# An attention, SwiGLU and bilinear kernel: front for the first batch alone, pack and unpack both one batch ahead

## The chip, the cores and the metric

The kernel runs on one core of one Trainium2 chip. TensorE (PE in the rows, PEld for its weight loads) multiplies, VectorE (DVE), ScalarE (ACT) and GpSimd (POOL) do the element-wise work, SyncE (SP) issues the DMAs. Each engine works through its own list of instructions in the written order and waits on semaphores for the others. The metric is the device time of one execution in microseconds (us), the median of several runs; less is better. A profiled execution gives the trace of every instruction.

## The reference

Three layers, one after the other, all outputs in fp32:

```python
def sm_attn(qq, kk, vv):
    s = scale * np.matmul(qq, kk.transpose(0, 1, 3, 2))
    a = np.exp(s - np.max(s, axis=-1, keepdims=True))
    return np.matmul(a / (np.sum(a, axis=-1, keepdims=True) + 1e-09), vv)
p_packed = sm_attn(p, k, v)              # 8 batches, 8 heads, 32 packed rows, 576 tokens, 64 wide
x = sm_attn(q, p_packed, p_packed)       # back to 576 tokens; then x as (4608, 512)
xn = x / np.sqrt(np.mean(x * x, axis=-1, keepdims=True) + 1e-06) * rms_g
g, val = xn @ w_gate, xn @ w_val         # 512 -> 1536
x = (g / (1 + np.exp(-g)) * val) @ w_out # 1536 -> 512
out = ((x @ w1) * (x @ w2)) @ w3 @ w_out2
```

## The kernel before

**Stages.** The first third of the span does attention and the gate and value products, batch by batch, and writes their silu product `hT_d` to memory. The rest (from line 480 on: `w_out`, then the bilinear layer) reads it back; the diff does not touch it.

**What a batch needs.** `pack(b)` (line 170) is the first attention: scores (L181), maximum, Exp (L188), transposes of the weights (L197), the product with `v` (L208), a transpose of it (L220) and two small block-diagonal tiles, `bdP1T` (L224) and `bdG` (L239, made from L234). It has 7 steps; a step ends at each `yield`. `unpack(b)` (line 246) is the second attention: scores against the packed rows (L262), a block transpose on VectorE (L266), maximum (L272), subtraction (L274), Exp on ScalarE (L275), sum (L278), a multiply by the reciprocal on GpSimd (L281), a transpose back (L285), then the sum of squares for the norm (L292, L295, L298, L304) and its reciprocal root (L310, L315, L318), and at last the split of the normed rows into two halves of fp32r precision, `ah` and `al` (the helper of L55 and L56). It has 18 steps. `unpack(b)` needs all of `pack(b)`.

**The dense part.** `dense_units(b)` (line 356) has 48 units. A unit is six matmuls of 128x288 (L376) into one of four PSUM banks `gv`. Units go in pairs: the even one is the gate, whose bank ScalarE reads with Tanh (L382) and VectorE multiplies by one plus that (L383); the odd one is the value, which ScalarE copies (L387) and GpSimd multiplies in (L388). After units 3, 11, 19, 27, 35 and 43 comes `wb_unit` (L337): 8 matmuls that fold the packed rows into the next 256 columns of the weights, and their split into `wbh` (ScalarE) and `wbl` (VectorE), two of each, in turns.

**What sets the order.** It is written out by hand. `planned` runs `dense_units(b)` and after the unit with number n takes one step of `unpack` or `pack` for each n in the tables `UNPACK` and `PACK`. In the loop before, `unpack(b + 1)` and `pack(b + 2)` run beside `dense_units(b)`: packing is two batches ahead, so beside the last loop of this kind, b = 6, there is no packing left. The front, ahead of the first dense loop, takes the steps of `pack(0)`, `pack(1)`, `unpack(0)`, the first `wb_unit` and conversions in the order of a string of letters.

**Conversions.** The weights arrive as 64-bit floats. `convert` makes fp32 of a 128x512 piece: ScalarE takes the high words (L108) and the low words (L109), VectorE shifts (L111) and merges (L112), GpSimd adds (L114). The gate and value weights `w_gv` are 24 such pieces, 512 KB each as loaded; `wb_unit(b, g)` of the first batch needs the first 4(g + 1) of them. Pieces of `w_out` are converted later, two in each loop from b = 1 on. `c_h` and `c_y` have two buffers each. Loads go through SP's queue in the written order; `k` and `q` have two buffers, `v` one, the 64-bit pieces four.

## Time and profile before

| | us |
|---|---|
| median of 3 runs | 1455.12 (1455.07 to 1457.11) |
| the profiled execution, its own time | 1451.91 |
| span of the profiled execution, first to last instruction | 1450.1 |
| TensorE busy in it | 1360.0 (94%) |
| VectorE, ScalarE, GpSimd busy | 795.9, 546.7, 489.9 |
| chain that ended last: TensorE's share of the span | 75% |

Over the whole span TensorE is the engine to look at. The 40 slices of the page, 36 us each, show where it is not busy: in the first two (4 and 5 tenths, then 7), and in a slice at about 480 us (7 tenths). A matmul counts as busy from its start to a modelled end, so idle time of TensorE is read from gaps between matmuls and from windows, not from the busy share alone. Times within the trace are counted from the start of the span.

### The profile page before, as it was taken

What the parts mean: (1) busy time and instruction counts of PE and PEld (TensorE: products, weight loads), DVE (VectorE), ACT (ScalarE), POOL (GpSimd) and SP (SyncE); (2) the same over time, 40 slices, a digit from 0 to 9 for tenths busy, and PEclk for the clock granted to TensorE, in tenths of its full rate; (3) what the DMA queues carried; (4) which work ended last, traced back from release to release, by engine and by line L of the source; (5) the groups of instructions that cost most, each with busy time, mean ns of one, the idle gap of its engine ahead of it and who ended that gap; (6) DMA issues with size and microseconds to landing.
All of it is one profiled execution on the core that took longest, in us unless ns stands there. A gap on an engine that the chain in (4) does not pass through costs nothing.

```text
span 1450.1 us, 22603 instructions
## 1 busy us (share of the span) xinstructions
PE 1360.0 (94%) x8824; PEld 1121.8 (77%) x8824; DVE 795.9 (55%) x1267; ACT 546.7 (38%) x1080; POOL 489.9 (34%) x438
## 2 busy tenths in 40 slices
PE   4579999999999899999999978999999999999988
PEld 2368878778788788888887756888788788788877
DVE  4787576666766557736358844335334433533343
ACT  3455455555555555624245532113112211311211
POOL 2456445445456542201034503322221222222111
PEclk9689999999999999999999999999999999999999
DMA  9854453444222466726349885442642633444263
GB/s 308 296 186 119 160 186 120 154 153 141 75 96 81 153 211 236 229 98 201 121 161 364 313 307 225 167 149 84 238 146 88 237 141 115 179 142 145 92 254 125
DMA packets 65562, 253.65 MB, mean 175 GB/s; under 512 B 7344, under 2 KB 7344, under 8 KB 55344
## 3 DMA queue, kind: packets, MB, share of 16 engines
q1 hardware_dynamic: 65456, 252.21, 49.5%
q8 instruction: 69, 1.13, 0.3%
q14 instruction: 37, 0.30, 0.1%
HBM read 185.08 MB, written 67.11 MB: 174 GB/s over the span
## 4 chain that ended last, share of the span: by engine, by line
PE 75%; DVE 8%; DMA 5%; ACT 3%; issue 3%; POOL 1%; SPq 1%; ACTq 0%; DVEq 0%; POOLq 0%
PE gv L799 22%; PE gv L376 17%; PE at L566 8%; PE gv L772 7%; PE at L772 7%; PE gv L566 6%; PE at L337 2%; DMA hr<-w_d 2%; DMA w<-ws_d 2%; PE at L657 2%; PE gv L657 2%; DVE stage L56 1%; PE at L292 1%; DVE c_t L111 1%; DVE th L383 1%
## 5 line engine op out<-in xcount | busy, mean ns | idle before, releaser
L799 PE MATMUL gv<-xh,w 128*128 128x512 f32 (+1 forms) x1120 | 288.7, 373 | 13.5 <-DMA w<-ws_d 6.1
L55 ACT ACTIVATE hh<-hr 128x512 fp32r<-128x512 f32 (+1 forms) x148 | 91.2, 618 | 421.1 <-DVE hr L767 332.9
L799 PEld LDWEIGHTS gv<-xh,w 128*128 128x128 f32 x1120 | 201.9, 190 | 53.3 <-DMA w<-ws_d 7.4
L388 POOL TENSOR_TENSOR ht<-th,vl 128x288 f32<-128x288 f32 x192 | 163.8, 861 | 178.6 <-ACT vl L387 97.6
L376 PE MATMUL gv<-ah,wbh 128*128 128x288 f32 x768 | 178.6, 314 | 15.9 <-ACT vl L387 12.4
L56 DVE TENSOR_TENSOR hl<-hr,hh 128x512 fp32r<-128x512 f32 (+1 forms) x148 | 140.4, 951 | 63.2 <-ACT hh L55 60.2
L376 PEld LDWEIGHTS gv<-ah,wbh 128*128 128x128 f32 x768 | 122.7, 191 | 67.6 <-issue 27.8
L826 POOL TENSOR_TENSOR u<-u,c 128x512 f32<-128x512 f32 (+1 forms) x40 | 63.5, 1587 | 323.5 <-DVE u L767 323.5
L376 PE MATMUL gv<-al,wbh 128*128 128x288 f32 x768 | 167.2, 299 | 0.0
L767 DVE TENSOR_TENSOR hr<-gv,hr 128x512 f32<-128x512 f32 (+1 forms) x80 | 51.1, 639 | 209.4 <-PE gv L799 209.4
L376 PE MATMUL gv<-ah,wbl 128*128 128x288 f32 x768 | 165.5, 297 | 0.0
L799 PE MATMUL gv<-xl,w 128*128 128x512 f32 (+1 forms) x560 | 162.3, 372 | 0.0
L114 POOL TENSOR_TENSOR c_o<-c_o,c_y 128x512 int32<-128x512 int32 x52 | 72.9, 1402 | 223.1 <-DVE c_o L112 200.6
L376 PEld LDWEIGHTS gv<-al,wbh 128*128 128x128 f32 x768 | 125.1, 190 | 1.1 <-DVE al L56 0.9
L376 PEld LDWEIGHTS gv<-ah,wbl 128*128 128x128 f32 x768 | 124.8, 190 | 0.0
L383 DVE SCALAR_TENSOR_TENSOR th<-th,gv 128x288 f32<-128x288 f32 x192 | 84.3, 445 | 63.1 <-ACT th L382 62.1
L799 PEld LDWEIGHTS gv<-xl,w 128*128 128x128 f32 x560 | 102.6, 191 | 18.4
L566 PE MATMUL at<-hh,wo_h 128*128 128x512 f32 x240 | 94.7, 394 | 7.3 <-ACT hh L55 7.3
L387 ACT ACTIVATE vl<-gv 128x288 f32<-128x288 f32 x192 | 79.3, 413 | 58.5 <-PE gv L376 57.2
L56 DVE TENSOR_TENSOR wbl<-at,wbh 128x512 fp32r<-128x512 f32 x96 | 65.9, 687 | 60.3 <-ACT wbh L55 59.6
L566 PE MATMUL at<-hl,wo_h 128*128 128x512 f32 x240 | 94.8, 395 | 2.3 <-DVE hl L56 2.1
L382 ACT ACTIVATE th<-gv 128x288 f32<-128x288 f32 x192 | 79.4, 413 | 42.9 <-PE gv L376 42.9
(131 smaller groups left out, 2416.2 us busy)
## 6 DMA issues: line engine op xcount, KB each, us to landing
w<-ws_d SPq DMA_DIRECT2D x40, 1792.0 KB, 7.4
hT_d<-ht SPq DMA_DIRECT2D x96, 288.0 KB, 2.5
hr<-hT_d SPq DMA_DIRECT2D x108, 256.0 KB, 4.4
ws_d<-stage SPq DMA_DIRECT2D x16, 896.0 KB, 8.3
w<-in_w_gv_dram SPq DMA_DIRECT2D x24, 512.0 KB, 7.0
w<-in_w_out_dram SPq DMA_DIRECT2D x20, 512.0 KB, 4.5
v<-in_v_dram SPq DMA_DIRECT2D x8, 1152.0 KB, 7.6
q<-in_qT_dram SPq DMA_DIRECT2D x8, 1152.0 KB, 7.0
```

What stands on the lines that cost most here:

```text
L55: nc.scalar.activation(out=hi, in_=src, func=AF.Copy)
L56: eng_lo.tensor_tensor(out=lo, in0=src, in1=hi.bitcast(F32), op=ALU.subtract)
L114: nc.gpsimd.tensor_tensor(out=d, in0=d, in1=shape(y), op=ALU.add)
L376: nc.tensor.matmul(t[:, :HALF], lhsT=w[:, e, 256 * i + 128 * f:256 * i + 128 * f + 128], rhs=x[:, e, HALF * hf:HALF * hf + HALF], start=(n ...
L382: nc.scalar.activation(out=th, in_=t[:, :HALF], func=AF.Tanh, scale=0.5)
L383: nc.vector.scalar_tensor_tensor(out=th, in0=th, scalar=1.0, in1=t[:, :HALF], op0=ALU.add, op1=ALU.mult)
L387: nc.scalar.activation(out=vl, in_=t[:, :HALF], func=AF.Copy, scale=0.5)
L388: nc.gpsimd.tensor_tensor(out=ht[:, hf], in0=th, in1=vl, op=ALU.mult)
L566: nc.tensor.matmul(acc[m], lhsT=w[:, kk, 128 * m:128 * m + 128], rhs=x, start=(kk == 0 and a == 0), stop=(kk == NF - 1 and a == 2))
L772: nc.tensor.matmul(acc[m], lhsT=x[:, 128 * m:128 * m + 128], rhs=w[i], start=(i == 0 and n == 0), stop=(i == 7 and n == 2))
L799: nc.tensor.matmul(t, lhsT=wi[:, r, j, a], rhs=x[b][:, j, r, :w], start=(start and n == 0), stop=(n == 5), skip_group_check=True)
L826: nc.gpsimd.tensor_tensor(out=u2, in0=u2, in1=c22, op=ALU.mult)
```

## The change

Five things change, all in the attention and dense stage. Line numbers below are of the kernel before; in the one after, everything from `convert` on stands 4 to 24 lines later.

1. A conversion is two steps: `widened` (the two ScalarE instructions) and `joined` (the two of VectorE and the one of GpSimd). For `w_gv` they are called apart, by `gv_widen` and `gv_join`; a widened piece waits in `c_h` and `c_y`. `wb_unit` no longer converts what is missing, it takes it as converted.
2. The front has only `pack(0)`, `unpack(0)` and the first `wb_unit`, with 9 pieces widened and 8 joined; the letters a and b stand for these two.
3. `pack(b + 1)` runs beside `dense_units(b)`, ahead of `unpack(b + 1)` in the same loop, with new tables; the loop b = 6 has a `pack` now. The 16 joins left run at even distances in the first dense loop. The two conversions of `w_out` in each later loop move from units 21 and 35 to 26 and 38.
4. Loads: two pieces of `w_gv` instead of three ahead of `v`, `k(b + 2)` in every `pack`, `q(b + 1)` right behind `v(b + 1)` in `pack(b)`.
5. An Exp on a 128x2 tile at the start, so that ScalarE's table is loaded there.

```diff
-    def convert(dst, w, shape):
+    def widened(w):
...
         nc.scalar.activation(out=h, in_=w[:, :, 1].bitcast(F32), func=AF.Copy, scale=float(2.0 ** -112))
         nc.scalar.activation(out=y, in_=w[:, :, 0].bitcast(U32), func=AF.Copy, scale=float(2.0 ** -29))
+        return h, y
+
+    def joined(dst, hy, shape):
+        h, y = hy
...
+    def gv_widen():
+        i = len(gvhy)
+        if i < len(GV):
+            gvhy.append(widened(gv64[i]))
+            gv_load(1)
...
-        if b:
-            load_k(b + 2)
+        load_k(b + 2)
...
         load_v(b + 1)
+        load_q(b + 1)
...
-        while not all((g, c) in converted for c in range(NC)):
-            next(gvw)
+        assert all((g, c) in converted for c in range(NC))
...
-    next(gvw)
+    gv_load(2)
     load_v(0)
     load_q(0)
+    gv_load(2)
     load_k(1)
+    warm = att.tile([128, 2], F32, name="warm")
+    nc.scalar.activation(out=warm, in_=ones, func=AF.Exp)
...
-    front = dict(p=chained(pack(0), pack(1)), u=unpack(0), c=gvw, w=wb_first(), l=later())
-    for x in "pp c c p c pp c pp u c u u p u p u c w u u u c u uu p u c uu l pp c uu c uu pp c l c c":
...
+    front = dict(p=pack(0), u=unpack(0))
+    for x in "a pp b a p b pp pp u uu uu aa uu b u b u uu a u w b a u u b a uu uu b a b a":
...
-    PACK = [8, 8, 16, 31, 32, 40, 43]
-    UNPACK = [0, 1, 3, 4, 6, 11, 13, 15, 17, 24, 24, 25, 31, 32, 40, 41, 42, 44]
+    PACK = [0, 0, 8, 10, 10, 12, 16]
+    UNPACK = [17, 18, 18, 19, 20, 21, 22, 23, 24, 32, 33, 33, 37, 37, 41, 42, 43, 44]
...
-        others = [(UNPACK, unpack(b + 1))]
-        if b + 2 < B:
-            others.insert(0, (PACK, pack(b + 2)))
+        others = [(PACK, pack(b + 1)), (UNPACK, unpack(b + 1))]
```

**Where instructions move.** Three places. First VectorE in the front, from the product with `v` to the first transposes of `unpack(0)`; `c_t` and `wgv` are a conversion's two VectorE instructions, `p` is the packed product, `bdP1T`, `gP1T` and `bdG` the small tiles of `pack(0)`, `a` the scores of `unpack(0)`. Before:

```order
L216 TENSOR_SCALAR p_243<-at,rs 128x64 x2
L111 TENSOR_SCALAR c_t<-c_h 128x512
L112 SCALAR_TENSOR_TENSOR wgv<-c_h,c_t 128x2x256
L224 COPY bdP1T<-at 64x4x32 x2
L226 TENSOR_TENSOR gP1T<-at,gT 128x128
L239 COPY bdG<-at 32x2x32 x4
L266 STREAM_TRANSPOSE a_275<-at 128x2x288 x2
```

The same place after:

```order
L241 TENSOR_SCALAR p_241<-at,rs 128x64 x2
L249 COPY bdP1T<-at 64x4x32 x2
L251 TENSOR_TENSOR gP1T<-at,gT 128x128
L264 COPY bdG<-at 32x2x32 x4
L291 STREAM_TRANSPOSE a_263<-at 128x2x288 x2
```

The conversion between `p` and `bdP1T` is gone from the chain.

Second VectorE in a later dense loop, b = 2 before and b = 1 after, where the scores of `unpack` are worked on: `a` the scores, `mx` their maximum, `rs` their sum, `th` the gate of a unit, `wbl` the split of a `wb_unit`. Before:

```order
L266 STREAM_TRANSPOSE a_2307<-at 128x2x288 x2
L272 TENSOR_REDUCE mx_2308<-a_2307 128x18
L383 SCALAR_TENSOR_TENSOR th<-th,gv 128x288
L274 TENSOR_TENSOR a_2307<-a_2307,mx_2308 128x576
L56 TENSOR_TENSOR wbl<-at,wbh 128x512 x2
L383 SCALAR_TENSOR_TENSOR th<-th,gv 128x288
L272 TENSOR_REDUCE mx_2308<-a_2307 128x18
L383 SCALAR_TENSOR_TENSOR th<-th,gv 128x288
L274 TENSOR_TENSOR a_2307<-a_2307,mx_2308 128x576
```

After:

```order
L291 STREAM_TRANSPOSE a_1703<-at 128x2x288 x2
L405 SCALAR_TENSOR_TENSOR th<-th,gv 128x288
L295 TENSOR_REDUCE mx_1704<-a_1703 128x18
L297 TENSOR_TENSOR a_1703<-a_1703,mx_1704 128x576
L295 TENSOR_REDUCE mx_1704<-a_1703 128x18
L56 TENSOR_TENSOR wbl<-at,wbh 128x512 x2
L405 SCALAR_TENSOR_TENSOR th<-th,gv 128x288
L297 TENSOR_TENSOR a_1703<-a_1703,mx_1704 128x576
L301 TENSOR_REDUCE rs_1705<-a_1703 128x18
```

There are two gates of units between the first maximum and the second subtraction's end where three stood, and three passes over the scores stand in a row ahead of the `wbl` of a `wb_unit`.

Third ScalarE at the same two places; `a` is the Exp of half of the scores, `vl` the value of a unit, `wbh` the split of a `wb_unit`. Before:

```order
L382 ACTIVATE th<-gv 128x288
L387 ACTIVATE vl<-gv 128x288
L275 ACTIVATE a_2307<-a_2307 128x576
L55 ACTIVATE wbh<-at 128x512 x2
L382 ACTIVATE th<-gv 128x288
```

After:

```order
L404 ACTIVATE th<-gv 128x288
L298 ACTIVATE a_1703<-a_1703 128x576
L409 ACTIVATE vl<-gv 128x288
L55 ACTIVATE wbh<-at 128x512 x2
L404 ACTIVATE th<-gv 128x288
L298 ACTIVATE a_1703<-a_1703 128x576
L409 ACTIVATE vl<-gv 128x288
```

The first Exp now stands ahead of the value of unit 19 as well as of the split, and the second one follows behind the gate of unit 20, where it came three units after the split before (units 4, 5 and 6).

## Rows read from the trace of the kernel before

**Rows 1.** Windows: length, busy us of PE, PEld, DVE, ACT, POOL, PEclk, DMA share, GB/s.

```profile
0.00:64.05 64.05, 27.29 (x388) 15.42 (x388) 37.83 (x71) 23.30 (x41) 20.73 (x25) 0.83 0.84 286
64.05:136.36 72.31, 62.60 (x606) 51.19 (x600) 57.37 (x105) 41.65 (x93) 42.72 (x41) 0.89 0.54 183
136.36:425.19 288.83, 279.45 (x2997) 233.78 (x2996) 188.19 (x384) 153.33 (x364) 139.18 (x154) 1.00 0.42 139
425.19:476.78 51.59, 51.09 (x444) 43.19 (x443) 32.89 (x62) 28.80 (x69) 27.85 (x31) 1.00 0.21 80
70.77:107.41 36.64, 27.46 (x215) 21.63 (x213) 29.59 (x52) 20.62 (x46) 20.57 (x20) 0.86 0.60 201
107.41:123.74 16.33, 15.84 (x212) 13.91 (x220) 13.15 (x24) 10.37 (x25) 13.44 (x14) 1.00 0.34 93
...
79.40:86.20 6.80, 5.39 (x44) 3.67 (x45) 5.13 (x8) 3.56 (x9) 3.00 (x3) 0.50 0.64 193
```

**Rows 2.** Timeline of the front: start, duration, engine, line, what [idle before <-releaser].

```profile
10.46 1.28 ACT L188 ACT_TABLE_LOAD   x1 [10.46 <-DVE nb L186]
...
18.23 2.79 PE L208 MATMUL at<-v,a1T 96*32 96x64 f32 x96 [2.73 <-DVE a1T L199]
...
24.66 0.66 ACT L108 ACTIVATE c_h<-w 128x512 f32<-128x512 f32 x1 [7.21 <-DMA w<-in_w_gv_dram]
...
26.42 0.60 DVE L224 COPY bdP1T<-at 64x128 f32<-64x128 f32 x2
...
27.44 2.38 PE L262 MATMUL at<-q,bdP1T 64*32 64x288 f32 x32
...
44.83 4.27 PE L292 MATMUL at<-a2T,bdG 128*128 128x288 f32 x8 [7.18 <-DVE a2T L285]
...
57.07 1.22 PE L315 MATMUL at<-ident,rinv 96*128 96x96 f32 x6 [2.99 <-POOL rinv L310]
...
70.77 0.46 DVE L383 SCALAR_TENSOR_TENSOR th<-th,gv 128x288 f32<-128x288 f32 x1
```

**Rows 3.** DMA issues of the first 64.05 us: count, KB each, median us to landing.

```profile
w<-in_w_gv_dram SPq DMA_DIRECT2D x15, 512.0 KB, 9.2
v<-in_v_dram SPq DMA_DIRECT2D x3, 1152.0 KB, 12.7
```

**Rows 4.** A merge on VectorE while GpSimd adds, from the timeline of the front.

```profile
15.62 1.64 DVE L112 SCALAR_TENSOR_TENSOR wgv<-c_h,c_t 128x512 int32<-128x512 int32 x1
```

**Rows 5.** Groups of 70.77 to 123.74, VectorE: count, busy us, mean ns, idle before.

```profile
L112 DVE SCALAR_TENSOR_TENSOR wgv<-c_h,c_t 128x512 int32<-128x512 int32 x11 | 9.9, 902 | 0.4
...
L111 DVE TENSOR_SCALAR c_t<-c_h 128x512 int32<-128x512 int32 x11 | 6.1, 558 | 3.2 <-ACT c_h L108 3.1
```

**Rows 6.** Waits of TensorE from 136.36 to 425.19 (five dense loops): us, times, longest.

```profile
PE at L337 <- ACT e L188: 6.1, 5, 1.5
PE gv L376 <- ACT vl L387: 3.0, 5, 0.6
```

**Rows 7.** Groups of the loop from 367.70 to 425.19: count, busy us, mean ns.

```profile
L56 DVE TENSOR_TENSOR wbl<-at,wbh 128x512 fp32r<-128x512 f32 x12 | 8.2, 686 | 7.6 <-ACT wbh L55 7.5
...
L274 DVE TENSOR_TENSOR a<-a,mx 128x576 f32<-128x576 f32 x2 | 1.5, 750 | 0.0
L55 ACT ACTIVATE wbh<-at 128x512 fp32r<-128x512 f32 x12 | 7.2, 597 | 7.7 <-DVE wbl L56 5.6 <-PE at L337 2.2
...
L275 ACT ACTIVATE a<-a 128x576 f32<-128x576 f32 x2 | 1.4, 686 | 2.3 <-DVE a L274 2.3
L281 POOL TENSOR_TENSOR a<-a,rs 128x576 f32<-128x576 f32 x2 | 2.3, 1162 | 0.8 <-DVE rs L280 0.8
```

**Rows 8.** Timeline of TensorE in a dense loop without gaps: one unit and the next one's start.

```profile
440.34 0.42 PE L376 MATMUL gv<-ah,wbh 128*128 128x288 f32 x2
...
441.12 0.43 PE L376 MATMUL gv<-ah,wbh 128*128 128x288 f32 x2
```

**Rows 9.** Timeline of TensorE in the first dense loop: its longest gap.

```profile
80.81 0.85 PE L376 MATMUL gv<-ah,wbh 128*128 128x288 f32 x2 [4.38 <-ACT vl L387]
```

## What the change will do to the time: the prediction

> **What bounds the kernel now.** I read the windows by stage first, then the timeline of the front, then TensorE's waits in the dense loops, and last the groups that give durations. Three stages behave differently. In the five dense loops from 136.36 to 425.19 TensorE is busy 279.45 of 288.83 us at a granted clock of 1.00: it is the bound, idle for only 9.38 us, and what it does there cannot be hidden [rows 1]. In the front, up to its first dense matmul at 64.05, it is busy 27 us; what counts is one chain through all engines, as well as what stands between its links [rows 1, 2]. From there to about 107 the first dense loop is held by VectorE: in 70.77 to 107.41 it is busy 29.59 of 36.64 us, and TensorE stops up to 4.38 us for a PSUM bank that waits behind it [rows 1, 9]. The change shortens the front, loads the loop that VectorE holds, and moves TensorE's work into a loop that TensorE bounds. So the sum has four terms. It is made against the profiled execution's own time, 1451.91; the median of the runs is 3.2 higher, and I add the difference to the median. About 0.2%, 2.9 us, is what a measurement of this kernel tells from no change.
>
> **Term 1, the front.** I follow the chain of `pack(0)` and `unpack(0)` to the first gate product (L383), which stands at 70.77 [rows 2].
> The table: 1.28 us stood between the first maximum and the first Exp, now it lies in the idle front. That is 1.3 off the chain, if the product with `v` can use it. The Trainium skill (ScalarE: Activation LUTs, What ACT_TABLE_LOAD costs) puts a switch of sets at 2.66 us with its drain; by that figure the front could gain up to 1.4 more and the whole sum would be +3.3. No row here shows such a drain. The product stood at 18.23, waiting for a copy; `v`, issued at about 4 behind three weight pieces, takes 12.7 to land, so it was there by 16.8 [rows 2, 3]. One piece of 512 KB less ahead of it is 1.8 us at the 286 GB/s of the front [rows 1], so 15.0 to 16.8; with a join and the table gone the copy is done by 14, so I take 15.5. L208 then ends at 18.3.
> From the end of L208 (21.02) to `bdP1T` (26.42) before, VectorE stood behind a conversion whose ScalarE half waited 7.21 us for its load [rows 2]. That join is out of the way; the packed product and its transpose take about 1.1, so `bdP1T` starts at 19.4, and L262 a microsecond later as before, at 20.5: 6.9 earlier.
> From L262 to L292 it was 17.4 us, with a maximum, an Exp and two conversions of others between [rows 2]. Now: 2.4 for L262, nine passes of VectorE over the scores at about 0.75, one Exp at 0.69, one GpSimd multiply at 1.16 [rows 7], one join at 1.1 to 1.6 and half of the passes overlapped by L262 and GpSimd: 11 us, so L292 at 31.5. From there to L315 it was 12.2, part of it the transposes of `pack(1)`; the new order puts `wbl` and one join ahead of the small step that feeds GpSimd, so I take 13.5: L315 at 45. From L315 to the first gate product it was 13.7 with `pack(1)`'s tail and four joins; now two joins, the norm's multiply and the split: 7.6. The gate product comes at 52.6 instead of 70.77: **18.2 earlier**. The loads keep up at the old 286 GB/s: up to the ninth piece they are 9 of 512 KB, 7 of `k`, `v` and `q` at 1152 KB and another 512 KB, 13.5 MB, 47 us [rows 1, 3].
>
> **Term 2, the rest of the first dense loop.** At its first gate product before, 13 joins were done and 11 left; now it is 8 and 16. Five joins are added to the stretch in which VectorE is the bound. Eleven took 9.9 + 6.1 us there, 1.45 each, so +7.3 [rows 5]; most merges are longer than they would be alone, since one that GpSimd's add overlaps reads 1.64 [rows 4]. The tail of `pack(1)` adds 1.6. From 70.77 to 123.74 (gate of unit 34) VectorE was busy 29.59 + 13.15 = 42.7, so now 51.6 up to the same place. The separate widening takes away the 3.1 us in which it waited for ScalarE's half [rows 5], so I take its busy share as 29.59 / (36.64 - 3.1) = 0.88: 58.6 us, ending at 111.2 where it was 123.3. Behind it the last `wb_unit` waits for the last join, then TensorE leads as before. So terms 1 and 2 together give **-12**. Ends: at the old share of 0.81 the stretch takes 63.9 us and the gain is 7; at 0.95 it takes 54.3 and the gain is 16.4.
>
> **Term 3, the later dense loops.** Before, the nine idle microseconds of five loops were two stalls of each, 1.0 to 1.5 for a slot that the Exp of `pack` reads, and 0.6 [rows 6]. With `pack` at units 0 to 16 and no unpacking beside it, that Exp is through before unit 3 ends: both stalls go. In their place I expect stalls where `unpack` now stands, one step per unit from 17 to 24. Count from the last copy of `bdG`, at 0, which stands behind the gate of unit 16 and frees the slot of L262's second half (about 0.3 of idle). TensorE: L262's half to 0.55, unit 18 to 1.35, unit 19 to 2.15 at 0.78 each [rows 8], `wb_unit` (1.05) to 3.2. VectorE: two transposes to 1.4, the gate of 18, which waits for its Tanh, at 2.4, then maximum and subtraction at 0.75 each to 3.9. ScalarE: the Exp (0.69) to 4.6, the value of 19 to 4.9, and only then `wbh`, at 4.8 where it could have been at 3.25. The split is 0.60, 0.69, 0.60, 0.69 in turns [rows 7] and ends at 7.4; the gate of unit 20 follows on VectorE at 7.8, and unit 24, which wants that bank, could have started at 6.4: 1.4 idle. The second subtraction and Exp (0.75 + 0.69) hold the value of 21 until 9.5, and unit 25 wants its bank at 8.6: 0.9 idle. With 0.2 at the reciprocal root, for which there are now 4 units, a loop has 2.8. The conversion at unit 26 stands on VectorE ahead of `wbl` behind the late second transpose (it waits for GpSimd's 1.16); I put 1.0 for it, in the five loops that have it. So 2.8 + 5 x 3.8 = 21.8 for the loops 1 to 6, where 9.4 + 0.5 were [rows 1]: **+11.9**. Ends: no idle at all, -9.9; twice the two main stalls, +25.
>
> **Term 4, the seventh loop's packing.** TensorE was busy 279.45 / 5 = 55.9 a loop with a `pack` beside it and 51.09 in the one without [rows 1]. The latter now has one: **+4.8**, with nothing to hide it, as TensorE was busy 51.09 of 51.59 there. The loads that moved are early by whole loops and cost nothing; the wait for `v`'s one buffer in SP's queue holds back pieces that are wanted more than 10 us later.
>
> **Sum**: -12 + 11.9 + 4.8 = **+4.7**: 1456.6 by the profiled execution, 1459.8 by the median.
>
> **Rivals.** (a) *The stalls do not come, faster.* The four banks, or a VectorE that is quicker by the gaps I left, let TensorE run over the dense steps from 17 to 24. Each loop then idles as before, 1.9, the seventh too, so term 3 is +1.4: -12 + 1.4 + 4.8 = -5.8, 1449.3; with the low end of term 2, 1444.9. It decides at a `wbh` that is late by less than half a microsecond. For it: at units 3 and 4 before, an Exp stood ahead of `wbh` too, and no wait of TensorE shows there [rows 6]. Against it: that Exp came behind the value, and its inputs two units earlier.
> (b) *The clock falls.* Two stalls of 1.4 and 0.9 follow each other within 3 us. The granted clock was 0.50 in 79.40 to 86.20, behind a gap of 4.38 [rows 1, 9], and 1.00 over all five loops with their shorter ones. If every one of six loops lost 3.4 us to half clock, half the length of that window, each would cost 1.7: +10, 1470.
> The Trainium skill (TensorE: Matmul & The Clock Gate, A second HAM failure mode: psum-queue depth-cycling) says that short idles between groups of matmuls that cycle through PSUM banks can make the clock swing. By that rule (b) would come; the five loops, which idle in this way at clock 1.00, speak against it.
> (c) *The first loop gains less.* VectorE works at its old share, or pieces land late and ScalarE, in order, holds `ah` behind one. Terms 1 and 2 give -7: +9.7, 1464.8.
> (d) *The change doesn't do what it says*: the table is loaded a second time when the first real Exp comes, or a join is late for its `wb_unit`. The first costs 1.3, the second the 1.3 to 1.6 of a join at most; neither changes the sign by itself, and I leave it within the range.
>
> **How the numbers follow.** Forecast 0.40 (slower 0.26, within 0.12, faster 0.02), since its own range is about +0.5 to +9; (a) 0.37 (faster 0.32, within 0.05); (b) 0.09 (slower); (c) 0.14 (slower 0.09, within 0.05). Faster 0.34, same 0.22, slower 0.44. The range leaves out a tenth on each side: 1444 (rival (a) with the better end of term 2) to 1468 (between (c) and (b)); the forecast's own is 1455.5 to 1464.
>
> **What the profile after should show.** First gate product near 53; a VectorE busy share near 0.9 to about 110; the second loop starting near 124 instead of 136.4. In each later loop no wait of L337 for the Exp of `pack`, and two gaps of about 1.4 and 0.9 at units 24 and 25. A seventh loop of near 59 instead of 51.6. Wrong would be: loops of 56 or less, a granted clock below 1.00 in them, or a second loop that starts later than 130.

## The result and the profile after

The median went from 1456.11 us (1455.07 to 1457.72) to **1468.86** (1465.55 to 1470.87): a ratio of 1.0084, interval 1.0062 to 1.0106. The change makes the kernel 12.75 us slower, 0.8%. The forecast was slower too, but by 4.7, and its range ended at 1468.

The profiled execution has a span of 1469.1 where before it was 1450.1. Of these 19 us, 15.1 are there by the last matmul of the dense part (542.67, before 527.60). The other 3.9 stand in the part behind it, whose code is the same: in the 14 profiles of this document it took between 922.5 and 926.4, before the least and after the most of them. So the difference of two traces is not that of the medians, and the stages are compared by their own starts. The start of a loop is its first dense matmul; the first gate product is VectorE's:

| | before | after | difference | forecast |
|---|---|---|---|---|
| first gate product | 70.77 | 54.79 | -16.0 | -18.2 |
| second dense loop starts | 136.36 | 131.31 | -5.05 | -12 |
| its length and that of the loops 3 to 6, summed | 288.83 | 299.73 | +10.9 | +8.6 |
| the seventh loop (no packing before) | 51.59 | 59.73 | +8.1 | +8.1 |
| sum at the end of the seventh loop | 476.78 | 490.77 | +14.0 | +4.7 |

(In the forecast, 2.8 + 4 x 3.8 - 9.4 = 8.6 of term 3 falls on the five loops and 3.8 - 0.5 on the seventh, where term 4 adds 4.8. Loops are counted from one here; the expectations below call the first one loop 0 in places, so that their loops 1 to 6 are the second to the seventh.) Windows by stage, in the columns of [rows 1]: length, busy us of PE, PEld, DVE, ACT and POOL, granted clock, DMA share, GB/s. First the front and the first dense loop, the second, a later one and the seventh:

```profile
0.00:49.61 49.61, 20.39 (x231) 11.42 (x231) 26.74 (x50) 15.58 (x27) 15.16 (x21) 0.92 0.86 294
49.61:131.31 81.70, 67.34 (x599) 52.41 (x600) 65.10 (x110) 48.45 (x103) 47.27 (x45) 0.90 0.50 168
131.31:191.39 60.08, 58.00 (x599) 48.19 (x599) 36.90 (x76) 30.36 (x72) 25.81 (x30) 0.97 0.48 159
...
371.31:431.04 59.73, 56.76 (x599) 46.73 (x600) 38.12 (x78) 31.27 (x74) 27.12 (x31) 1.00 0.38 127
431.04:490.77 59.73, 56.76 (x599) 46.73 (x599) 38.12 (x78) 31.27 (x74) 27.06 (x31) 1.00 0.18 70
```

The front is 14.4 us shorter, and the first loop gives back most of that: 81.70 against 72.31. Every later loop is 59.7 or more where 57.5 was the rule, and the seventh is as long as the others.

**The front.** Timeline, in the columns of [rows 2]:

```profile
0.73 1.28 ACT L454 ACT_TABLE_LOAD   x1 [0.73 <-PEq L900]
...
10.62 0.74 ACT L213 ACTIVATE e<-at,nb 128x576 f32<-128x576 f32 x1
...
16.67 2.79 PE L232 MATMUL at<-v,a1T 96*32 96x64 f32 x96 [2.31 <-DMA v<-in_v_dram]
...
20.70 0.61 DVE L249 COPY bdP1T<-at 64x128 f32<-64x128 f32 x2 [0.71 <-PE at L245]
...
33.51 2.26 PE L315 MATMUL at<-a2T,bdG 128*128 128x288 f32 x4 [9.40 <-DVE a2T L308]
...
46.83 1.22 PE L338 MATMUL at<-ident,rinv 96*128 96x96 f32 x6 [5.04 <-POOL rinv L333]
...
54.79 0.46 DVE L405 SCALAR_TENSOR_TENSOR th<-th,gv 128x288 f32<-128x288 f32 x1 [0.50 <-ACT th L404]
```

(L315 here is the L292 of the kernel before, and L338 its L315.) Each link stands 1.2 to 2.2 behind the forecast (15.5, 19.4, 31.5, 45, 52.6): the product with `v` now waits for `v`, which is there at 16.67 and not at 15.5, and the rest follows it. The table is loaded once, in the idle front, and the first Exp comes 0.11 behind its bias.

**A later loop.** What TensorE waits for in the loops 3 to 7, from 191.39 on: us in total, times, longest. It stands against [rows 6]:

```profile
PE gv L398 <- ACT vl L409: 7.6, 10, 0.9
PE gv L398 <- DVE th L405: 7.2, 5, 1.8
```

The waits for the Exp of packing are gone, as forecast, and three others have come. (Between the first maximum and the second subtraction one gate of a unit stands in the loop after, as the rows of the change show, and not two, as the text under them says.) The timeline of one loop, units 20 to 25 (L398 a unit's matmuls, L404 and L405 the gate's Tanh and product, L409 the copy of a value, L55 and L56 the split of the `wb_unit`):

```profile
398.34 0.69 ACT L298 ACTIVATE a<-a 128x576 f32<-128x576 f32 x1 [2.05 <-DVE a L297]
...
398.93 0.39 ACT L409 ACTIVATE vl<-gv 128x288 f32<-128x288 f32 x1
...
399.22 0.59 ACT L55 ACTIVATE wbh<-at 128x512 fp32r<-128x512 f32 x1
...
400.57 0.60 ACT L55 ACTIVATE wbh<-at 128x512 fp32r<-128x512 f32 x1 [0.76 <-DVE wbl L56]
...
401.06 0.41 ACT L404 ACTIVATE th<-gv 128x288 f32<-128x288 f32 x1
...
401.81 0.44 DVE L405 SCALAR_TENSOR_TENSOR th<-th,gv 128x288 f32<-128x288 f32 x1
...
402.31 0.54 PE L398 MATMUL gv<-ah,wbh 128*128 128x288 f32 x2 [1.28 <-DVE th L405]
...
402.96 0.68 ACT L298 ACTIVATE a<-a 128x576 f32<-128x576 f32 x1 [1.49 <-DVE a L297]
403.55 0.39 ACT L409 ACTIVATE vl<-gv 128x288 f32<-128x288 f32 x1
...
403.99 0.54 PE L398 MATMUL gv<-ah,wbh 128*128 128x288 f32 x2 [0.62 <-ACT vl L409]
```

This is the chain of the prediction: Exp, value of unit 19, then the split, then the Tanh of unit 20, whose bank unit 24 wants (1.28 idle; 1.77 and 1.56 in the loops 3 and 4); then the second Exp ahead of the value of unit 21, whose bank unit 25 wants (0.62). A third gap of 0.88 follows at unit 32.

**The first loop.** The gate products of units 0, 14, 34 and the next loop's first stand at 70.77, 98.69, 123.29 and 138.16 before, and at 54.79, 78.41, 116.81 and 133.10 after (their starts; 123.74 in the prediction is the end of that gate). So up to unit 14 the new kernel is 4.3 faster, and between 14 and 34 it is 13.8 slower. The windows of units 14 to 34, the first of the kernel before, the second after:

```profile
98.69:123.29 24.60, 23.51 (x269) 20.56 (x267) 20.66 (x37) 15.20 (x33) 19.34 (x20) 0.98 0.54 176
```

```profile
78.41:116.81 38.40, 28.52 (x197) 21.50 (x195) 34.34 (x56) 21.62 (x45) 24.56 (x23) 0.87 0.50 174
```

Before, TensorE led there (23.51 busy of 24.60). After, VectorE is the busy one, 34.34 of 38.40, but not to the end. The same stretch cut at the gate of unit 28 (108.98):

```profile
78.41:108.98 30.57, 20.69 (x140) 14.59 (x139) 27.14 (x45) 17.11 (x35) 19.57 (x18) 0.84 0.60 205
108.98:116.81 7.83, 7.83 (x59) 6.91 (x57) 7.20 (x13) 4.52 (x11) 4.99 (x5) 0.95 0.14 53
```

Up to unit 28 VectorE leads, behind it TensorE does again. TensorE's waits from 54.79 to 116.81 mostly end where VectorE's queue does, directly (the gate, `bdG`) or through an engine that waits for it (L287 are the scores of `unpack`, L359 is `wb_unit`, L232 the product with `v`; L106 and L107 are ScalarE's two instructions of a conversion and L118 GpSimd's add):

```profile
PE gv L398 <- ACT vl L409: 3.6, 2, 1.9
PE at L287 <- DVE bdG L264: 3.1, 1, 3.1
PE at L359 <- POOL wgv L118: 3.1, 2, 2.5
PE at L232 <- ACT c_h L106: 2.2, 1, 2.2
PE gv L398 <- DVE th L405: 1.9, 1, 1.9
```

### The profile page after: what moved, and what is told of

It is laid out like the page before. It is cut to its first block, busy times and chain, and to the rows that moved or that the text cites. A ratio compares the mean times of both kernels' runs of the same rounds, so it can differ in the third digit from the quotient of the medians.

```text
span 1469.1 us, 22565 instructions
## 1 busy us (share of the span) xinstructions
PE 1372.7 (93%) x8824; PEld 1126.2 (77%) x8824; DVE 800.1 (54%) x1267; ACT 549.9 (37%) x1081; POOL 482.8 (33%) x438
## 4 chain that ended last, share of the span: by engine, by line
PE 76%; DVE 9%; DMA 6%; ACT 4%; issue 3%; POOL 1%; SPq 1%; ACTq 0%; DVEq 0%; POOLq 0%
PE gv L823 22%; PE gv L398 17%; PE at L590 8%; PE gv L796 7%; PE at L796 7%; PE gv L590 6%; PE at L359 2%; DMA hr<-w_d 2%; DMA w<-ws_d 2%; PE at L681 1%; PE gv L681 1%; DVE stage L56 1%; DVE c_t L115 1%; DVE wbl L56 1%; DVE hl L56 1%
## 5 line engine op out<-in xcount | busy, mean ns | idle before, releaser
L55 ACT ACTIVATE hh<-hr 128x512 fp32r<-128x512 f32 (+1 forms) x148 | 91.2, 618 | 425.3 <-DVE hr L791 334.1
L410 POOL TENSOR_TENSOR ht<-th,vl 128x288 f32<-128x288 f32 x192 | 159.3, 838 | 216.1 <-ACT vl L409 140.6
L398 PE MATMUL gv<-ah,wbh 128*128 128x288 f32 x768 | 184.0, 321 | 28.7 <-ACT vl L409 16.2
L398 PEld LDWEIGHTS gv<-ah,wbh 128*128 128x128 f32 x768 | 124.2, 193 | 84.8 <-issue 30.9
L56 DVE TENSOR_TENSOR hl<-hr,hh 128x512 fp32r<-128x512 f32 (+1 forms) x148 | 141.0, 955 | 62.9 <-ACT hh L55 60.2
L398 PE MATMUL gv<-al,wbh 128*128 128x288 f32 x768 | 169.1, 301 | 0.0
L398 PE MATMUL gv<-ah,wbl 128*128 128x288 f32 x768 | 166.9, 299 | 0.0
L118 POOL TENSOR_TENSOR c_o<-c_o,c_y 128x512 int32<-128x512 int32 x52 | 72.9, 1401 | 219.0 <-DVE c_o L116 196.8
L398 PEld LDWEIGHTS gv<-al,wbh 128*128 128x128 f32 x768 | 127.2, 193 | 1.3 <-DVE al L56 0.8
L398 PEld LDWEIGHTS gv<-ah,wbl 128*128 128x128 f32 x768 | 126.1, 192 | 0.0
L405 DVE SCALAR_TENSOR_TENSOR th<-th,gv 128x288 f32<-128x288 f32 x192 | 85.2, 447 | 75.0 <-ACT th L404 69.7
L56 DVE TENSOR_TENSOR wbl<-at,wbh 128x512 fp32r<-128x512 f32 x96 | 66.2, 689 | 73.8 <-ACT wbh L55 73.8
L409 ACT ACTIVATE vl<-gv 128x288 f32<-128x288 f32 x192 | 78.9, 411 | 64.1 <-PE gv L398 56.9
L404 ACT ACTIVATE th<-gv 128x288 f32<-128x288 f32 x192 | 78.8, 410 | 49.8 <-PE gv L398 49.3
```

The costliest lines, as they stand in the source:

```text
L55: nc.scalar.activation(out=hi, in_=src, func=AF.Copy)
L56: eng_lo.tensor_tensor(out=lo, in0=src, in1=hi.bitcast(F32), op=ALU.subtract)
L118: nc.gpsimd.tensor_tensor(out=d, in0=d, in1=shape(y), op=ALU.add)
L398: nc.tensor.matmul(t[:, :HALF], lhsT=w[:, e, 256 * i + 128 * f:256 * i + 128 * f + 128], rhs=x[:, e, HALF * hf:HALF * hf + HALF], start=(n ...
L404: nc.scalar.activation(out=th, in_=t[:, :HALF], func=AF.Tanh, scale=0.5)
L405: nc.vector.scalar_tensor_tensor(out=th, in0=th, scalar=1.0, in1=t[:, :HALF], op0=ALU.add, op1=ALU.mult)
```

## The experiments

The first two change one table of the kernel after and ask where the stalls of the later loops come from.

**e1: the dense steps spread out.**

```diff
-    UNPACK = [17, 18, 18, 19, 20, 21, 22, 23, 24, 32, 33, 33, 37, 37, 41, 42, 43, 44]
+    UNPACK = [17, 18, 21, 22, 23, 24, 25, 26, 28, 32, 33, 33, 37, 37, 41, 42, 43, 44]
```

> The kernel after, with only the table of unpacking steps changed: steps 3 to 9 at units 21, 22, 23, 24, 25, 26, 28 instead of 18, 19, 20, 21, 22, 23, 24, so that no subtraction and Exp stands in the queues ahead of the split of the wb_unit behind unit 19. Theory (the two stalls of 1.28 and 0.62 us at units 24 and 25 come from that Exp and subtraction): both go in each of the loops 1 to 6, the loops are 57.8 to 58.0 instead of 59.7, and the total is 11 us below the kernel after (about 1458). Rival (VectorE and ScalarE just have too much between units 17 and 32, so the same wait comes a few units later): stalls of about the same sum at units 26 to 34, loops of 59 or more, total within 3 us of the kernel after.

Measured: 1488.33 us (1485.79 to 1490.56), 19 above the kernel after; the loops 3 to 7 take 62.6 to 63.8, the second 61.2. Both theories failed by the total. The stalls at units 24 and 25 went, so their cause was right. But larger ones took their place, where the rival had put them: 0.58 at unit 31 and 3.00 at unit 32 (1.42 in the second loop, which has no conversion at 26). The timeline of a loop there:

```profile
298.36 0.77 DVE L308 STREAM_TRANSPOSE a2T<-a 128x576 f32<-128x576 f32 x1
...
299.04 0.90 DVE L115 TENSOR_SCALAR c_t<-c_h 128x512 int32<-128x512 int32 x1
...
299.98 0.69 DVE L116 SCALAR_TENSOR_TENSOR c_o<-c_h,c_t 128x512 int32<-128x512 int32 x1
300.59 0.68 DVE L56 TENSOR_TENSOR wbl<-at,wbh 128x512 fp32r<-128x512 f32 x1
...
301.31 0.60 ACT L55 ACTIVATE wbh<-at 128x512 fp32r<-128x512 f32 x1 [4.03 <-DVE wbl L56]
...
302.57 0.85 PE L398 MATMUL gv<-ah,wbh 128*128 128x288 f32 x2 [3.00 <-ACT vl L409]
```

The late transpose and the conversion of `w_out` stand on VectorE ahead of `wbl`; ScalarE waits 4.03 for it with Tanh and values queued behind, and TensorE 3.00. The granted clock of these loops is 0.95 to 0.97: it is at its lower level, 1.2 GHz, for 3.4 or 6.8 us in each of them, beginning inside that gap (at 302.3, 363.8, 428.6, ...).

**e2: the conversion of unit 26 moved to 30.**

```diff
-            others.append(([26, 38], some(ow, 2)))
+            others.append(([30, 38], some(ow, 2)))
```

> The kernel after, with only the first w_out conversion of a loop moved from unit 26 to unit 30. Theory (the stall of 0.88 us at unit 32 is that conversion's, which stands on VectorE ahead of wbl): it goes in the five loops that have it, which become 58.8 instead of 59.7; the stalls at units 24 and 25 stay at 1.28 and 0.62; total 4.4 us lower, about 1464.5. Rival (the stall comes from the late second transpose, which waits for GpSimd): 0.6 to 0.9 stay at unit 32 and the total is within 2 us of the kernel after.

Measured: 1465.84 (1463.82 to 1470.07). The gap at unit 32 is gone from all five loops; those at units 24 and 25 stay. TensorE's waits in the loops 2 to 7 of e2:

```profile
PE gv L398 <- DVE th L405: 8.2, 6, 1.7
PE gv L398 <- ACT vl L409: 4.5, 10, 0.6
```

The theory holds: the loops without a fall of the clock are 59.0 to 59.4. Two others had one of 3.4 us and took 60.0. (It is the gaps that show it: the medians are 3.0 apart, and the two kernels' times overlap.)

**e3: the kernel before with the small Exp alone.**

```diff
     load_k(1)
+    warm = att.tile([128, 2], F32, name="warm")
+    nc.scalar.activation(out=warm, in_=ones, func=AF.Exp)
```

> The kernel before, with only the small Exp at the start, so that ScalarE's table of 1.28 us is loaded in the idle front. Theory (it is 1.3 us of the front's chain, and VectorE then holds the first loop): first gate product 0.5 to 1.3 earlier than 70.77, second loop 0 to 1.3 earlier than 136.36, total 0 to 1.3 us below the kernel before. Rival (the table is loaded again when the first real Exp comes, as the copies between use another one): a second table load of 1.28 in the trace and no gain.

Measured: 1454.55, ratio 0.9996 (0.9985 to 1.0008). One table load, at 0.73, and the first Exp 1.0 earlier (10.75), but the first gate product at 71.59 instead of 70.77: the gain is lost ahead of it, and neither theory came as written. By itself this part is worth nothing that can be measured.

**e4: the new front with the old loops.**

```diff
...
-    front = dict(p=pack(0), u=unpack(0))
-    for x in "a pp b a p b pp pp u uu uu aa uu b u b u uu a u w b a u u b a uu uu b a b a":
...
+    front = dict(p=pack(0), u=unpack(0), n=pack(1), l=later())
+    for x in "a pp b a p b pp pp l u uu uu aa uu nn u b u b uu a u w b a u u l n b a uu n uu b a n l b a":
...
-    PACK = [0, 0, 8, 10, 10, 12, 16]
-    UNPACK = [17, 18, 18, 19, 20, 21, 22, 23, 24, 32, 33, 33, 37, 37, 41, 42, 43, 44]
+    PACK = [8, 8, 16, 31, 32, 40, 43]
+    UNPACK = [0, 1, 3, 4, 6, 11, 13, 15, 17, 24, 24, 25, 31, 32, 40, 41, 42, 44]
...
-        others = [(PACK, pack(b + 1)), (UNPACK, unpack(b + 1))]
+        others = [(UNPACK, unpack(b + 1))]
+        if b + 2 < B:
+            others.insert(0, (PACK, pack(b + 2)))
+        if b == 0:
+            others = [([0, 1], front["n"]), ([8, 8, 16, 31, 32, 40, 43], pack(2)),
+                      ([2, 3, 5, 6, 7, 11, 13, 15, 17, 24, 24, 25, 31, 32, 40, 41, 42, 44], unpack(1))]
...
```

> The front of the kernel after (table load, separate conversions, the chain of the first batch ahead), but packing two batches ahead again: the first four steps of pack(1) stand in gaps of the front, and from the second loop on tables, loads and conversions are those of the kernel before. Theory (the change loses its 14 us by 476.78 in the later loops and the seventh's packing, and gains 5 to the second loop): first gate product 54 to 58, second loop at 130 to 135, the loops 1 to 5 57.6 each, the sixth 51.6, total 1450 to 1454. Rival (packing of two batches in front and first loop eats the gain): second loop at 138 or later, total 1457 or more.

Measured: **1448.4** (1445.82 to 1451.17), ratio 0.9952 (0.9934 to 0.9969): faster than both kernels. First gate product 53.63, second loop at 129.71. The sixth and the seventh loop, in windows:

```profile
360.64:418.16 57.52, 55.85 (x600) 46.77 (x599) 37.70 (x78) 30.83 (x74) 28.11 (x31) 1.00 0.25 90
418.16:469.77 51.61, 51.11 (x443) 43.21 (x442) 32.88 (x62) 28.77 (x69) 27.85 (x31) 1.00 0.21 80
```

From the second to the sixth, 129.71 to 418.16, they take 288.45 us where [rows 1] has 288.83, and the seventh 51.61 for 51.59. So nearly all of the 20 us between this kernel and the one after belongs to packing one batch ahead with its tables (the places of the `w_out` conversions among them), not to the front. The first steps of `pack(1)`, five of them by the letters n (the expectation says four), cost the front nothing: its first gate product came at 53.63, and at 52.5 to 55.3 in the seven profiles of the new front without them.

**e5: a third buffer for the low words.**

```diff
-        y = cv.tile([128, 512], I32, tag="c_y", name="c_y", bufs=2)
+        y = cv.tile([128, 512], I32, tag="c_y", name="c_y", bufs=c_y_bufs[0])
...
-    c_o_bufs = [2]
+    c_o_bufs, c_y_bufs = [1], [3]
...
```

> The kernel after, with three buffers instead of two for c_y, the low words of a conversion, in the attention and dense stage (c_o has one instead of two there, to make room). In the first dense loop of the kernel after, ScalarE waited 4.8 us in 8 places for GpSimd to release c_y (L107 behind wgv of L118), with the Tanh and the copy of the value queued behind it. Theory A (that blocked queue is what stretches the first loop): the waits go, the first loop is 3 to 5 us shorter than the 81.7 to 85.4 of the three profiles with this loop so far, so below 80, and the total 3 to 5 us lower. Theory B (VectorE's work is the bound there, its share was .85): the waits go, the first loop stays at 81 to 85 and the total within 2 us of the kernel after.

Measured: 1469.69 (1464.76 to 1471.46), first loop 82.62. (Of the three profiles that the expectation counts, e1's has another table in its first loop; 81.7 and 84.8 are the two of the same one.) ScalarE's waits for GpSimd at L107, 4.8 us in the kernel after, are gone, and it waits longer for TensorE instead (7.8 for a value's matmuls where it was 5.1). The loop is no shorter: theory B. ScalarE's blocked queue was a symptom.

**e6 and e9: four joins taken out of the first loop, at its end or in its middle.** They run in the second loop instead, and the `wb_unit` that needs them does not wait. e6 takes those at units 26, 28, 30 and 32:

```diff
...
-            others.append(([1, 3, 5, 7, 9, 12, 14, 16, 18, 20, 22, 25, 26, 28, 30, 32], joins()))
...
+            others.append(([1, 3, 5, 7, 9, 12, 14, 16, 18, 20, 22, 25], some(js, 12)))
...
+        elif b == 1:
+            others.append(([20, 24, 28, 32], some(js, 4)))
...
```

> The kernel after, with 4 of the 16 joins of the first loop (those of the last column group) taken out of it and run in the second loop at units 20, 24, 28 and 32. The last wb_unit of the first batch then reads the columns of the first group, so that part of the first batch's output is left wrong. Theory (each join in the first loop costs what VectorE takes for it there, 15.8 + 11.7 us for 16, 1.72 each): first loop 6.9 us shorter than 81.7 to 85.4, so 75 to 78.5; second loop up to 1 longer. Rival (it is GpSimd's chain and the wait of a wb_unit for the last join of its group that sets the time): more than 6.9 goes, above 9, since the waits of 2.5 and 0.5 before the wb_units go too. Second rival (the stalls are the dense steps' own): less than 3.

e9 takes those at units 18, 20, 22 and 25; so that the right pieces are left out, the last two column groups change places in the order of the joins:

```diff
...
-            others.append(([1, 3, 5, 7, 9, 12, 14, 16, 18, 20, 22, 25, 26, 28, 30, 32], joins()))
...
+            others.append(([1, 3, 5, 7, 9, 12, 14, 16, 26, 28, 30, 32], some(js, 12)))
...
+        elif b == 1:
+            others.append(([3, 7, 11, 15], some(js, 4)))
...
```

> The kernel after, with 4 of the 16 joins of the first loop taken out of the stretch in which unpack(1)'s dense steps stand: those at units 18, 20, 22 and 25, of the fifth column group, which run in the second loop at units 3, 7, 11 and 15. The fifth wb_unit of the first batch then reads the first group's columns, so that part of the first batch's output is left wrong. (In e6 the four joins at units 26 to 32 were taken out, and the gate of unit 34 came 61.4 us behind the first gate, where the kernel after has 62.0.) Theory (from unit 14 to 34 VectorE is the bound in the kernel after, busy 34.34 of 38.40 us, where in the kernel before TensorE was, 23.51 of 24.60): the four joins take 1.72 each from it and the wait of 2.53 for the last of them goes: the gate of unit 34 at 53 to 56 behind the first, second loop 6 to 9 earlier than 131.3 to 135.5. Rival (packing's and unpacking's own chain of links sets the time, the joins fill its gaps): gate of unit 34 at 59 to 62, second loop less than 3 earlier.

| | first gate to gate of unit 34 | to the next loop's first gate | first loop | median |
|---|---|---|---|---|
| after | 62.0 | 78.3 | 81.70 | 1468.86 |
| e6, four late joins out | 61.4 | 77.1 | 80.49 | 1466.86 |
| e9, four middle joins out | 54.8 | 71.1 | 74.46 | 1460.20 |

(e9's five times lie between 1459.17 and 1466.44, and the trace is of the fastest; the second loop, which takes the four joins, is 1.9 longer in e6 and 1.3 in e9.) Four joins are worth 0.6 us at units 26 to 32 and 7.2 at units 18 to 25, where VectorE works on unpacking's dense steps. The first loop varies from profile to profile, but ahead of unit 14: from there to unit 34 the kernel after, e2 and e5 take 38.40, 38.65 and 38.39. That stretch in e6, then in e9:

```profile
77.33:115.08 37.75, 28.62 (x184) 21.00 (x183) 28.04 (x48) 17.89 (x38) 20.32 (x21) 0.82 0.54 183
```

```profile
76.11:107.32 31.21, 25.20 (x197) 18.65 (x195) 27.41 (x47) 18.09 (x39) 18.93 (x19) 0.89 0.64 213
```

Against 34.34 in 38.40, VectorE is busy 6.3 less in e6 and the stretch only 0.6 shorter; in e9 it is busy 6.9 less and the stretch 7.2 shorter. So in the middle of the loop VectorE's time counts nearly in full, 1.8 us a join, and at its end it does not. One thing e9 does not separate: with the four joins go TensorE's waits of 2.5 and 0.5 for the last of them. e6 fell to its second rival, e9 bore out its theory. The stretch from the gate of unit 28 to the next loop's first gate in e6, which TensorE fills:

```profile
108.38:130.83 22.45, 22.38 (x198) 19.10 (x204) 11.51 (x23) 11.09 (x26) 11.07 (x13) 1.00 0.14 54
```

**e7: the kernel before, with steps that shared a place apart.** TensorE is busy 0.9 us longer in each loop after (56.76 against 55.85), beside its stalls; is that the number of places in which other matmuls break the dense stream?

```diff
-    PACK = [8, 8, 16, 31, 32, 40, 43]
+    PACK = [8, 8, 16, 29, 30, 38, 41]
```

> The kernel before, with the four last steps of packing at units 29, 30, 38 and 41 instead of 31, 32, 40 and 43, so that none of their matmuls stands next to another step's or a wb_unit's any more: the dense stream of the later loops is broken in 15 places instead of 12, as in the kernel after. Theory (the 0.86 us by which TensorE's busy time per loop is longer in the kernel after is the cost of three more breaks, 0.2 to 0.3 each): busy time per loop 56.5 to 56.8 instead of 55.85, the loops 1 to 5 0.7 to 0.9 longer if no new stall comes, total 3.5 to 4.5 above the kernel before. Rival (the 0.86 belongs to the order of the steps, as L287 waiting for its second half): busy 55.9, total within 1.5 us.

Measured: 1454.44, ratio 0.9992 (0.9974 to 1.0011). Two of its loops:

```profile
310.06:367.65 57.59, 55.80 (x600) 46.69 (x599) 37.88 (x78) 30.89 (x74) 28.18 (x31) 1.00 0.41 137
367.65:425.15 57.50, 55.90 (x600) 46.74 (x599) 37.85 (x78) 30.89 (x74) 28.05 (x31) 1.00 0.25 90
```

No: the theory falls. A part of the 0.9 is seen in the order of steps: L287 now starts right behind the copies of `bdG`, and its 32 matmuls take 1.56 from first to last where L262 took 1.20. The rest stays open.

**e10: e1 with the conversions at 34 and 40.**

```diff
-            others.append(([26, 38], some(ow, 2)))
+            others.append(([34, 40], some(ow, 2)))
```

> The kernel of the run e1_unpack_spread (steps 3 to 9 of unpacking spread to units 21 to 28), with the two w_out conversions of a loop at units 34 and 40 instead of 26 and 38. In e1 a stall of 3.0 us stood at unit 32 of the loops that have a conversion at 26, and one of 1.42 in the second loop, which has none. Theory (the conversion's two instructions stand with a late transpose ahead of wbl of the wb_unit behind unit 27): the 3.0 falls to 1.4 or less, the stall at unit 24 stays near 0.55, loops of 59.5 to 60.5 without a fall of the clock; total 1466 to 1472. If the spread had no price of its own beside that, the stall is below 0.5, the loops 57.8 to 58.3, total 1458. Rival (the chain is too late by itself, and L315 at unit 32 waits for its second transpose): a stall of 2 or more at unit 32, loops above 61.

Measured: 1478.05 (1474.05 to 1481.32), above the 1466 to 1472 expected. The stall of 3.00 fell to 1.43, so half of it was the conversion, and 0.68 stays at unit 31. The rest goes with the late transpose: in the third loop it starts at 234.38 ahead of `wbl`, and ScalarE's second `wbh` waits 3.52 for that. What the expectation left out is the clock. Two loops, one with a fall and one without:

```profile
320.06:382.02 61.96, 58.43 (x599) 47.94 (x600) 39.66 (x78) 31.05 (x74) 28.03 (x31) 0.97 0.42 141
382.02:442.11 60.09, 56.88 (x599) 46.67 (x600) 39.33 (x78) 31.02 (x74) 27.98 (x31) 1.00 0.37 126
```

Gaps of 0.68 and 1.43, 2.5 us apart, are followed by 3.4 us at 1.2 GHz in five of six loops, at 1.7 to 1.9 us each. In the kernel after, gaps of 1.28 and 0.62, 1.7 us apart, were followed by one fall in six. So the spread of unpacking over more units, which looks the gentler plan, is worse than the dense one: it brings the transposes to the `wb_unit` behind unit 27. The Trainium skill (TensorE: Matmul & The Clock Gate, A second HAM failure mode: psum-queue depth-cycling) says of one kernel that the short idles between its groups of matmuls, which cycle through PSUM banks, come often enough to make the clock swing. The loops of e10 agree (0.97), those of the kernel after from 191.39 on, with stalls of nearly the same sum (1.90 to 2.40 for 2.11), do not (1.00).

**e8, e11 and e12: can the first loop of e4 be made shorter?** The edits are shown against e4. e8 gives it three `c_y` buffers and earlier joins:

```diff
...
-            others.append(([1, 3, 5, 7, 9, 12, 14, 16, 18, 20, 22, 25, 26, 28, 30, 32], joins()))
+            others.append(([1, 2, 3, 5, 6, 8, 9, 11, 13, 14, 16, 18, 20, 22, 24, 26], joins()))
...
```

> The kernel of the run e4_front_two_ahead, with three c_y buffers (c_o one) and the 16 joins of the first loop at units 1, 2, 3, 5, 6, 8, 9, 11, 13, 14, 16, 18, 20, 22, 24, 26, so that no wb_unit should wait for the last join of its group (e4 waited 2.34, 3.81 and 0.47 us there). Theory (those waits end last): second loop at 123 to 126 instead of 129.71, total 1442 to 1445. Rival (the joins come earlier but VectorE's gates then come later, the loop's length is VectorE's sum): second loop at 128 to 132, total within 2 us of e4's 1448.4.

Measured: 1447.49 (1444.3 to 1448.82), ratio 0.9948 (0.9928 to 0.9968), second loop at 128.01. TensorE no longer waits for a join (6.6 us in e4), but 4.3 for gates instead: the rival. The wait for the Exp of `pack(2)` is still there (3.9). e11 does two more joins in the front and spreads the 14 left anew:

```diff
-    for x in "a pp b a p b pp pp l u uu uu aa uu nn u b u b uu a u w b a u u l n b a uu n uu b a n l b a":
+    for x in "a pp b a p b pp pp l u uu uu aa uu nn u b u b a uu b a u w b a u u l n b a uu b a n uu b a n l b a":
...
```

> The kernel of the run e4_front_two_ahead with two more joins in the front, 10 instead of 8, and the 14 left at units 2, 5, 8, 10, 12, 14, 17, 19, 21, 23, 26, 28, 30 and 32, none in the last unit ahead of a wb_unit. Theory (VectorE holds the first loop up to about unit 34, each join is 1.5 to 1.7 there, and in the front VectorE has gaps): first gate product at most 1.5 later than 53.63, second loop at 126 to 128 instead of 129.71, total 1445 to 1447. Rival (the front's chain takes the joins in full): first gate product 56 or later, second loop at 129 to 131, no gain.

Measured: 1448.93 (1448.33 to 1449.57); first gate product 55.66, so 2.0 later, second loop at 132.06. No gain, rather as its rival says. e12 packs late, with the joins a little earlier:

```diff
-            others = [([0, 1], front["n"]), ([8, 8, 16, 31, 32, 40, 43], pack(2)),
+            others = [([0, 1], front["n"]), ([27, 29, 33, 36, 37, 40, 43], pack(2)),
...
```

> The kernel of the run e4_front_two_ahead, with pack(2) late in the first loop (units 27, 29, 33, 36, 37, 40, 43 instead of 8, 8, 16, 31, 32, 40, 43) and the 16 joins at units 1, 2, 4, 6, 8, 10, 12, 14, 16, 18, 20, 22, 24, 26, 28, 30, done some units ahead of the wb_unit that needs them. Theory (VectorE holds the first loop up to about unit 34 and TensorE from there on, as the runs e6 and e9 showed for the kernel after; so VectorE's 1.8 us of maxima and the wait of up to 3.9 for the Exp of pack(2) go from where they count): the gate of unit 34 at 56 to 58.5 behind the first gate product instead of 61.7, second loop at 125 to 127.5 instead of 129.71, total 1443 to 1446. Rival (pack(2)'s matmuls and passes just move to the end of the loop, where TensorE has no room): gate of unit 34 earlier by as much, but second loop at 129 to 131, total within 2 us of e4's 1448.4.

Measured: 1447.51 (1446.63 to 1451.34), ratio 0.9962 (0.9952 to 0.9973), second loop at 128.92, the gate of unit 34 at 61.9 behind the first as in e4. Both theories missed: the waits moved. TensorE's two largest in that loop:

```profile
PE gv L400 <- DVE th L407: 6.9, 4, 3.4
PE at L361 <- ACT e L213: 3.7, 1, 3.7
```

The Exp of `pack(2)`, now behind unit 27, holds the slot that a `wb_unit` wants, as it did behind unit 8. All four kernels with the new front and packing two batches ahead are 0.4 to 0.5% faster than the kernel before; their first loops, from first gate to first gate, take 76.9 to 78.8 in every order, where the kernel before takes 67.4. They hold 16 or 14 joins and it holds 11; that this is the whole cause is not shown, for e11, with 14, is no shorter than the others.

## Why the prediction was wrong

The direction was right and so were the mechanisms of three of four terms. The size was wrong by 9.3 us at the end of the seventh loop: 2.2 in term 1, 4.8 in term 2 and 2.3 in terms 3 and 4. Two of the prediction's own signs of being wrong came, a second loop that starts later than 130 (131.31) and a granted clock below 1.00 in one of the later loops.

**Term 1** was nearly right: -16.0 for -18.2. `v` did not land earlier for one piece less ahead of it (the product at 16.67, before 18.23, now waits for nothing else), and between the first product (49.61) and the first gate (54.79) stood ScalarE's second half of a conversion and a step of packing at 1.2 GHz. A part of the 2.2 varies from profile to profile: in the six others with this front the first gate product stands at 52.5 to 55.3. The table's share is not seen in the end (e3), and no drain beside the 1.28 us is.

**Term 2 is the step that failed.** Its sum took one busy share of VectorE, 0.88, for the whole stretch up to unit 34, and let the loop give back 6.2 of the front's gain; it gave back 10.9. Up to the end of the gate of unit 34 the sum has 51.6 us of VectorE's work and so 58.6; measured are 62.45 (54.79 to 117.24), 3.8 more, and behind that gate 0.9 more than forecast was lost. (The 123.3 of the working is the start of that gate before; its end is 123.74.) VectorE was busy 52.88 of the 62.02 up to the start of that gate: 1.3 more work, at a share of 0.85, and 0.83 and 0.81 in the two other profiles with the same first loop (e5, e2), where the old share was 0.81. The 3.1 us in which VectorE waited for ScalarE's half of a conversion did go, as the working said. But its waits for `wbh`, ScalarE's half of a split, doubled. From 70.77 to 123.74 before, then from 54.79 to 116.81 after:

```profile
DVE wbl L56 <- ACT wbh L55: 2.7, 4, 0.7
```

```profile
DVE wbl L56 <- ACT wbh L55: 5.5, 7, 1.8
```

Where the loop lost its time is seen when the stretch is cut by units. First, before, VectorE held the loop at most to unit 14 (busy 21.64 of 27.92); from there to 34 TensorE was busy 23.51 of 24.60, and a row of the prediction had it already: 15.84 of 16.33 in 107.41 to 123.74 [rows 1]. There the kernel before had slack on VectorE. Second, the new table puts unpacking's first nine steps at units 17 to 24, among the joins, so that the part up to unit 28 is now VectorE's (27.14 of 30.57, a share of 0.89), while up to unit 14 its share is 0.79 (18.55 of 23.62) and behind unit 28 TensorE is busy all the time. The 0.88 of the sum fits the middle part alone. e9 shows the middle part by its other end: four joins less there give 7.2 us, and four less behind it (e6) 0.6. Third, a join costs 27.5 / 16 = 1.72, not 1.45. The shift is stretched beside GpSimd as well as the merge that [rows 4] shows. (The sum of the work came out only 1.3 too low all the same, in part because the two subtractions of `unpack`, 1.76 each in that stretch before, took 0.75 each.) Two joins in a row after, the first shift (64.06) begun 0.2 ahead of GpSimd's next multiply, the second (65.97) 0.2 behind the start of GpSimd's add for the first join (65.77, 1.29 long):

```profile
64.06 0.42 DVE L115 TENSOR_SCALAR c_t<-c_h 128x512 int32<-128x512 int32 x1
64.51 1.18 DVE L116 SCALAR_TENSOR_TENSOR wgv<-c_h,c_t 128x512 int32<-128x512 int32 x1
...
65.97 1.37 DVE L115 TENSOR_SCALAR c_t<-c_h 128x512 int32<-128x512 int32 x1
```

The Trainium skill (Advanced Engine Details and Errata, VectorE Performance Modes) says that GpSimd shares VectorE's second port, so that GpSimd's instructions and those of VectorE in a two-port mode interfere with or block each other. The 0.42 against 1.37 agrees in kind; in which mode the shift runs, no row here shows.
And the clock: in the other two profiles with the same first loop the second one started at 133.8 (e2) and 133.3 (e5), so the gain is 2.5 to 5 in these three. The extra 2.5 in e2 lies ahead of unit 14 (26.48 for 23.62), and more time at 1.2 GHz is its likely cause (27.0 us of its first loop, 15.7 in the kernel after); no run isolates it. Between the kernel before and the one after the clock is no rival for the rest: at 1.2 GHz their first loops spent 15.3 and 15.7 us.

**Term 3: right mechanism, smaller stalls, and a cost that was not seen.** The stalls came at units 24 and 25 in the order foretold, at 1.28 and 0.62 for 1.4 and 0.9, and the conversion's at 0.88 for 1.0; e1 and e2 each removed one cause and its stall. TensorE's idle time in the loops 2 to 7 is 17.8 instead of 21.8. But it was busy 0.9 longer in each, which the term had at nothing: 284.95 in five loops where 279.45 were, 1.3 of it from one fall of the clock (164.3 to 167.7). **Term 4** was right in kind: 51.59 without packing, and 51.61 in e4. With 0.9 on top, TensorE's busy time rose by 5.67, not 4.8. Terms 3 and 4 together gave 19.0 for 16.7.

**The rivals.** (a) did not come. (b), the clock, came in one loop of six, at 1.3; e1 and e10 show that it needed little more to come in nearly all, at 1.7 to 1.9 each, the price the rival gave. (c) is nearest to what happened, -5.05 for its -7, and VectorE's share of 0.81 to 0.85 is near its reason too; what it lacked is the price of a join and the new place of unpacking. (d) did not come as written, but its second half, a join late for its `wb_unit`, was there: 2.5 and 0.5 in the first loop. The range ended too low: (c) at 1464.8 with the unseen 0.9 in each of six loops is 1470.

## What to carry to other kernels

Before scaling a stretch by the busy share of the engine that holds it, cut it where the holder changes: here the last 20 of 34 units had belonged to another engine than the 14 ahead of them. (That a sum cut so would have come out nearer is argued, not tried.) Price work that moves by the place it lands in: four joins cost 0.6 us or 7.2, depending on whether VectorE or TensorE led there. And a chain placed a few units later is not gentler by itself; what counts is which in-order queue it meets next, so a spread plan (e1) was worse than the dense one, while putting the second batch's packing into the gaps of the front (e4) kept the front's gain and the old loops.

## What the runs showed of the hardware

The clock's fall does not hang on the sum of the gaps in a loop alone. Gaps of 1.28 (up to 1.77) and 0.62 us, then 0.88 eight us later, left the granted clock at 1.00 in all five loops from 191.39 on of the kernel after, while 0.68 and 1.43 (e10) were followed by 3.4 us at 1.2 GHz in five loops of six. A stall of 2.1 us could so cost 3.9. Nor do like gaps always end alike: over the kernel after, e2, e5, e6 and e9, gaps of 1.3 to 1.8 and 0.6 came in 29 later loops, and the clock fell behind or between them in 8. What decides stays open; the gap of 1.43 in e10 also stands ahead of fp32 matmuls (L315), and no run separates that. The table load is 1.28 us with nothing else around it in the trace, and its removal from the chain is lost within the noise (e3).
